# Windowed attention into a routed two-layer MLP: the order of all work from a list schedule, and most matmuls on the full array

## The chip, the core and the metric

The kernel runs on one core of a Trainium2 chip. The engines are TensorE (PE, with its weight loads shown apart as PEld), VectorE (DVE), ScalarE (ACT), GpSimd (POOL) and SyncE (SP), each of which works through its own instructions in order; 16 DMA engines move data between the device memory and the on-chip memory. The metric is the device time of one execution in microseconds (us). Lower is better.

## What is computed

Eight batches, eight heads, 576 tokens, head size 64. Each token attends to the tokens at most 32 places away. The heads are laid side by side into x (576 x 512 for a batch), x is pooled over its tokens, a gate picks one of eight experts for the whole batch, and the expert's two matrices are applied.

```python
    scores = scale * np.matmul(q, k.transpose(0, 1, 3, 2))
    mask = np.abs(pos[:, None] - pos[None, :]) <= window
    scores = np.where(mask, scores, -1000000000.0)
    scores = scores - np.max(scores, axis=-1, keepdims=True)
    attn = np.exp(scores)
    attn = attn / (np.sum(attn, axis=-1, keepdims=True) + 1e-09)
    return np.matmul(attn, v).astype(np.float32)
    ...
    pooled = x.mean(axis=1)
    logits = pooled @ w_gate
    e_idx = np.argmax(logits, axis=1)
    ...
        h = np.maximum(x[mask] @ w1[e], 0.0)
        out[mask] = gate_w[mask, None, None] * (h @ w2[e])
```

The inputs are q, k, v (8 x 8 x 576 x 64, float32, 9.4 MB each) and the weights w1 (8 x 512 x 1024) and w2 (8 x 1024 x 512), of which each batch reads one expert: 2.1 MB of each.

## The kernel before

The loop at the end of the program runs over the batches b: `attention(b)`, then `moe` of batch b-1, then `gate` of batch b. A library of tiles gives out the buffers (rotating pools) and puts in the waits; within each engine the instructions stand nearly in the order of the text, with the neighbouring stages drawn together where the pools allow it.

`attention(b)` loads q, k and v with SP in pieces of 128 tokens (L134, L138); for each token and head one run of 64 floats, 256 bytes, is read. DVE casts q and k to bf16 and v to fp16 (L148 to L153). TensorE transposes q and k, two heads at a time, 128 tokens per transpose and 64 in the last (L162), and DVE copies the result out of PSUM (L167). The keys are cut into blocks of 128, 128, 128, 128 and 64. For each block the scores against its window of at most 192 queries are accumulated on top of a mask: a matmul with the identity writes the mask (L185, 352 or 480 columns, all 128 rows of the array), and matmuls on 64 rows of the array, one head on the upper and one on the lower half, add the scores (L194). ACT takes the exponential from PSUM into `etile` (L203). For each block of queries, `avp` collects the products with `vaug` (v and a column of ones, 65 columns) from up to three key blocks (L221); the neighbouring blocks give 32 queries each, so these matmuls use 32 columns of the array. DVE divides by the row sum (L232, L235), TensorE transposes the result (L245), ACT copies it into `xTt` (L250).

`gate` pools with a DVE reduction (L255), multiplies with `w_gate` (L261), and finds the expert with a few tiny DVE instructions. `moe` has SP read the expert's number (L302) and load the two matrices as float32 (L304, L308); DVE casts them to fp16 (L312, L314); TensorE does the first layer, 64 matmuls of 288 columns (L322 and L326, one half of the tokens each), ACT applies the relu (L330, L333), TensorE does the second layer, 40 matmuls of 512 columns (L340), ACT scales by the gate's weight (L347) and SP stores (L351).

## Time and profile before

| | |
|---|---|
| time, median of 3 runs | 389.33 us (384.39 to 390.08) |
| span of the profiled execution | 384.9 us |
| PE busy | 307.4 us (80%), 2656 matmuls |
| PEld busy | 176.6 us (46%) |
| DVE busy | 165.9 us (43%) |
| ACT busy | 153.8 us (40%) |
| POOL busy | 7.9 us (2%) |
| moved by DMA | 71.74 MB in 130861 packets, 113936 of them under 512 bytes |
| mean granted TensorE clock | 0.852 of full speed |

The profiled execution is one execution of its own; its span runs from its first to its last instruction, and the times of the runs are taken apart from it. A busy PE is not a PE at its peak: a matmul counts as busy from its issue to its modelled end, and the clock of TensorE is granted at one of two levels, full (2.4 GHz) or half (1.2 GHz). An engine's idle time costs only where the chain of work that ended last passes through it.

### The profile page before, as it was taken

How to read it: one execution, taken by the hardware profiler on the slowest of the kernel's cores; microseconds unless marked ns; L12 is line 12 of the kernel's file. 1: busy time of each engine (PE TensorE's matmuls, PEld its weight loads, DVE VectorE, ACT ScalarE, POOL GpSimd, SP SyncE). 2: the span in 40 equal slices, each digit the busy share in tenths (PEclk: the TensorE clock that was granted, in tenths of full speed). 3: DMA queues.
4: the chain of work that ended last, by engine and by line, in shares of the span. 5: the costliest groups of instructions: out<-in, count | busy, mean ns of one | idle time of the engine just before them, and what ended most of it. 6: DMA issues, size and time to landing. Idle time of an engine off the chain costs nothing.

```text
span 384.9 us, 6511 instructions
## 1 busy us (share of the span) xinstructions
PE 307.4 (80%) x2656; PEld 176.6 (46%) x2656; DVE 165.9 (43%) x349; ACT 153.8 (40%) x353; POOL 7.9 (2%) x31
## 2 busy tenths in 40 slices
PE   0397498699958997699969997799859995893395
PEld 0234244474445554475345554565337444551262
DVE  0634562651467153652476055633385046501310
ACT  1044126163622536153723455253716362352052
POOL 1400000000000000000000000000000000000000
PEclk9998558589995999599986997599978999598599
DMA  9999049905889189936897289927996495015803
GB/s 160 210 208 162 3 157 346 202 7 160 278 273 212 51 219 381 222 67 179 305 285 161 83 236 371 195 48 211 345 258 119 149 292 218 0 54 181 325 0 124
DMA packets 130861, 71.74 MB, mean 186 GB/s; under 512 B 113936, under 2 KB 113936, under 8 KB 130832
## 3 DMA queue, kind: packets, MB, share of 16 engines
q1 hardware_dynamic: 130832, 71.33, 70.6%
q8 instruction: 21, 0.34, 0.4%
q14 instruction: 8, 0.07, 0.1%
HBM read 61.88 MB, written 9.44 MB: 185 GB/s over the span
## 4 chain that ended last, share of the span: by engine, by line
PE 70%; DVE 17%; DMA 6%; issue 4%; POOL 1%; SPq 0%; ACT 0%; DVEq 0%; POOLq 0%; ACTq 0%
PE op L340 18%; PE hpa L322 11%; PE hpb L326 10%; PE tp L162 8%; PE spAB L185 7%; PE avp L221 6%; PE spAB L194 6%; DVE xs L235 5%; DMA w2s<-in_moe_w_dram 4%; DVE w1s L312 4%; DVE w2s L314 4%; PE xtp L245 4%; DMA w1s<-in_moe_w_dram 2%; DVE linv L232 2%; DVE kbf L148 1%
## 5 line engine op out<-in xcount | busy, mean ns | idle before, releaser
L322 PE MATMUL hpa<-xTt,w1s 128*128 128x288 f16 x256 | 77.3, 331 | 12.2 <-DVE w1s L312 12.2
L326 PE MATMUL hpb<-xTt,w1s 128*128 128x288 f16 x256 | 76.6, 328 | 0.0
L203 ACT ACTIVATE etile<-spAB 128x480 f16<-128x480 f32 (+1 forms) x128 | 54.7, 550 | 48.3 <-PE spAB L194 47.4
L340 PE MATMUL op<-w2s,hT 128*128 128x512 f16 (+1 forms) x320 | 71.3, 380 | 0.0
L245 PE MATMUL xtp<-id_f,xs 128*128 128x128 f16 (+1 forms) x160 | 25.1, 254 | 41.0 <-DVE xs L235 40.2
L250 ACT COPY xTt<-xtp 128x512 f16<-128x512 f16 (+1 forms) x40 | 21.7, 542 | 83.2 <-PE xtp L245 83.2
L340 PEld LDWEIGHTS <-hT 128*128 128x128 f16 (+1 forms) x320 | 31.4, 100 | 37.2 <-issue 3.4
L347 ACT ACTIVATE osb<-op,gwb 128x512 f32<-128x512 f32 (+1 forms) x40 | 27.4, 686 | 43.7 <-PE op L340 43.7
L221 PE MATMUL avp<-vaug,etile 128*32 128x65 f16 (+3 forms) x832 | 44.9, 212 | 0.0
L330 ACT ACTIVATE hT<-hpa 128x288 f16<-128x288 f32 x64 | 26.2, 410 | 42.7 <-PE hpa L322 42.7
L221 PEld LDWEIGHTS <-etile 128*32 128x32 f16 (+3 forms) x832 | 37.1, 110 | 5.8 <-issue 1.6
L322 PEld LDWEIGHTS <-w1s 128*128 128x128 f16 x256 | 28.6, 112 | 23.0 <-DVE w1s L312 12.3
L266 DVE COPY lg<-lgp 1x8 f32<-1x8 f32 x8 | 1.2, 154 | 86.3 <-PE lgp L261 86.2
L232 DVE RECIPROCAL linv<-avp 128x8 f32<-128x8 f32 (+1 forms) x40 | 8.1, 203 | 67.1 <-PE avp L221 67.1
L245 PEld LDWEIGHTS <-xs 128*128 128x128 f16 (+1 forms) x160 | 9.8, 104 | 55.8 <-DVE xs L235 52.6
L326 PEld LDWEIGHTS <-w1s 128*128 128x128 f16 x256 | 28.5, 111 | 10.5
L235 DVE TENSOR_TENSOR xs<-avp,linv 128x256 f16<-128x256 f32 (+1 forms) x80 | 30.1, 417 | 1.4
L194 PE MATMUL spAB<-qTs,kTs 64*128 64x192 bf16 (+2 forms) x320 | 29.0, 249 | 0.0
L162 PE MATMUL tp<-id_bf,qbf 128*128 128x128 bf16 (+1 forms) x160 | 17.3, 236 | 14.3 <-DVE qbf L148 12.8
L333 ACT ACTIVATE hT<-hpb 128x288 f16<-128x288 f32 x64 | 25.9, 405 | 0.0
L255 DVE TENSOR_REDUCE pooledT<-xTt 128x4 f32<-128x2304 f16 x8 | 20.4, 2553 | 11.3 <-ACT xTt L250 11.3
L194 PEld LDWEIGHTS <-kTs 64*128 64x128 bf16 (+1 forms) x320 | 11.4, 97 | 29.8 <-issue 27.0
(51 smaller groups left out, 220.3 us busy)
## 6 DMA issues: line engine op xcount, KB each, us to landing
w1s<-in_moe_w_dram SPq DMA_DIRECT2D x8, 2048.0 KB, 8.1
w2s<-in_moe_w_dram SPq DMA_DIRECT2D x8, 2048.0 KB, 13.3
raw_q<-in_q_dram SPq DMA_DIRECT2D x32, 256.0 KB, 7.3
raw_k<-in_k_dram SPq DMA_DIRECT2D x32, 256.0 KB, 5.2
raw_v<-in_v_dram SPq DMA_DIRECT2D x32, 256.0 KB, 3.6
out_dram<-osb SPq DMA_DIRECT2D x32, 256.0 KB, 2.2
raw_q<-in_q_dram SPq DMA_DIRECT2D x8, 128.0 KB, 5.1
raw_k<-in_k_dram SPq DMA_DIRECT2D x8, 128.0 KB, 4.9
```

The source lines that it names most:

```text
L162: nc.tensor.transpose(tp[:, SO[t] : SO[t] + ST[t]], src[0 : ST[t], t, 2 * hp : 2 * hp + 2, :], id_bf[0 : ST[t], 0 : ST[t]],)
L185: nc.tensor.matmul(sp[h][:, 0:mw], id_bf, ma, start=True, stop=False, skip_group_check=True,)
L194: nc.tensor.matmul(sp[h][0:J, off : off + RL[kb]], kTs[hoff : hoff + D, hp, KO[kb] : KO[kb] + J], qTs[hoff : hoff + D, hp, RLO[kb] : RHI[kb]],
L203: nc.scalar.activation(et[h][:, eo : eo + mw], sp[h][:, 0:mw], mybir.ActivationFunctionType.Exp, bias=0.0, scale=0.125,)
L221: nc.tensor.matmul(avp[pr : pr + m, base : base + 65], Es[h][0:J, EOFF[kb] + lo : EOFF[kb] + lo + m], vaug[0:J, kb, h, :], start=(ci == 0 ...
L235: nc.vector.tensor_tensor(xs[0:stl, bk * 256 : (bk + 1) * 256].rearrange("p (h4 d) -> p h4 d", h4=4), hv[:, bk, :, 0:64], linv[0:stl, bk, ...
L245: nc.tensor.transpose(xtp[:, dt, 0:stl], xs[0:stl, dt * P : (dt + 1) * P], id_f16[0:stl, 0:stl],)
L322: nc.tensor.matmul(hpa, lhs, xTt[:, dt, 0:N1A], start=(dt == 0), stop=(dt == NDT - 1),)
L326: nc.tensor.matmul(hpb, lhs, xTt[:, dt, N1A:S], start=(dt == 0), stop=(dt == NDT - 1),)
L330: nc.scalar.activation(hT[:, ft, 0:N1A], hpa, mybir.ActivationFunctionType.Relu)
L340: nc.tensor.matmul(op[0:stl, :], hT[:, ft, SO[t] : SO[t] + stl], w2s[:, ft, :], start=(ft == 0), stop=(ft == NFT - 1),)
L347: nc.scalar.activation(osb[0:stl, :], op[0:stl, :], mybir.ActivationFunctionType.Copy, bias=0.0, scale=gwb[0:stl],)
```

## The change

The kernel's body is written anew. Four things change.

**The order.** Every piece of work is an `Op` with an engine, a length put in by the author, the ops it waits for, the buffers it takes and frees, and a priority. `Plan.finish` runs once when the program is built: it keeps a clock for each engine and always emits the op that can start first (at equal time that of the lower priority), so that attention of later batches and the two layers of earlier ones are dealt out among each other. The priority of the layers of batch b is that of batch b + 1.4. The lengths decide the order only; on the chip every engine runs its list in order and waits on semaphores.

**The shapes.** Pairs of heads (h, h + 1) are laid behind one another, 1152 tokens that divide into nine full blocks of 128: all transposes of q and k are 128 x 128. The mask is no longer a matmul: the scores are written alone, ACT takes the exponential, and DVE multiplies with a mask of zeros and ones. `E` has blocks of zeros beside each band (the zero gaps), so that the products with v always use 128 stationary columns, two matmuls for each head and block of queries; the blocks of queries are shifted by 32. The pooling is 20 one-column matmuls. The last block of the second layer (64 tokens) runs as two halves of 256 columns side by side on 64 columns of the array each.

**Who does what.** q and k are loaded nine tokens to a partition (2304 bytes in one run), v as before in runs of 256 bytes, one DMA for each batch. POOL casts q, k and v (in batch 0 DVE casts k). The weights are loaded by POOL's own DMA queue, which converts them to fp16 on the way; the DVE casts are gone. Copies out of PSUM go to DVE or ACT, whichever the schedule finds free.

**The buffers.** All tiles live through the whole program and are handed on by the plan: 6 halves of raw q or k, 2 of raw v, 2 of `E`, 2 each of w1 and w2, 3 of the output, five PSUM banks for attention (`psA`) and three for the layers (`psM`).

The core of the diff; all of the old body (printed above) goes away.

```diff
--- before.py
+++ after.py
 ...
+    LAT = {"PE": 0.2, "ACT": 0.12, "DVE": 0.12, "SP": 0.0, "SW": 0.2}
+    DMA_GBS = 370.0
+    SOON = 0.08
 ...
+            if best is None:
+                raise RuntimeError(f"nothing can start: {[(e, [o.name for o in r]) for e, r in ready.items()]}")
+            _, t, op, eng = best
+            for e in op.eng.split("/"):
+                ready[e].remove(op)
+            op.eng = eng
+            left -= 1
+            for res, n in op.takes:
+                have = sorted(self.free[res], key=lambda h: h[:2])
+                got, self.free[res] = have[:n], have[n:]
+                op.got[res] = [g[2] for g in got]
+                held[(op.name, res)] = got
+            op.emit(op)
+            end = at[op.eng] = t + op.dur
+            over = end + self.LAT[op.eng]
+            if op.land:
+                dma_at = max(dma_at, end + 1.3) + op.land / (self.DMA_GBS * 1e3)
+                over = dma_at + 0.7
 ...
+    buffers("raw", [P, 2, J, D], FP32, 6)
+    buffers("qkb", [P, J, 2, D], BF16, 4)
+    qTs = buffers("qT", [P, 2 * QPAD + 2 * S], BF16, 4)
+    buffers("kT", [P, 2 * S], BF16, 4)
+    vraws = buffers("vraw", [P, 36, D], FP32, 2)
+    vaugs = buffers("vaug", [P, 36, D + 1], FP16, 2)
+    Es = buffers("E", [P, H, EH], FP16, 2)
+    buffers("xs", [P, DM], FP16, 7)
+    buffers("xT", [P, NDT, S], FP16, 3)
+    buffers("w1", [P, NDT, F], FP16, 2)
+    buffers("w2", [P, NFT, DM], FP16, 2)
+    buffers("hT", [P, S], FP16, 9)
+    buffers("osb", [P, DM], FP32, 3)
+    banks = [ps.tile([P, 512], FP32, name=f"bank{i}") for i in range(8)]
+    plan.resource("psA", banks[0:5])
+    plan.resource("psM", banks[5:8])
 ...
+                    nc.sync.dma_start(
+                        t.rearrange("p h j d -> p h (j d)"),
+                        src[b, 4 * quad : 4 * quad + 4]
+                        .rearrange("(h x) s d -> (x s d) h", h=2)
+                        .rearrange("(p r) h -> p h r", p=P),
+                    )
+                plan.add("SP", 0.6, f"ld{name}{b}{quad}", load, takes=[("raw", 1)],
+                         deps=[f"W2{b - 2}_"] if b > 1 else [],
+                         land=650e3, prio=base + quad)
 ...
+                    t = op.got["qkb"][0]
+                    (nc.vector if op.eng == "DVE" else nc.gpsimd).tensor_copy(
+                        t, raw[(b, quad, name)].rearrange("p h j d -> p j h d")
+                    )
+                    raw[(b, quad, name)] = t
+                plan.add("DVE" if b == 0 and name == "k" else "SW", 1.2, f"c{name}{b}{quad}", cast,
 ...
+            vr_of[b] = t
+            nc.sync.dma_start(
+                t, v[b].rearrange("h s d -> (h s) d").rearrange("(j p) d -> p j d", p=P)
 ...
+                        bank_of[tn] = bank
+                        pv = bank.bitcast(BF16).rearrange("p (j c) -> p j c", c=P)
+                        for j in range(j0, j1):
+                            nc.tensor.transpose(
+                                pv[:, j - j0, :], raw[(b, quad, name)][:, j], id_bf
+                            )
+                    plan.add("PE", 0.056 * (j1 - j0), tn, tr,
+                             deps=[f"c{name}{b}{quad}"] + ([f"T{b}{quad}{name}0"] if part else [])
+                             + (["ca"] if b == 0 else []),
 ...
+                        bank_of[sn] = bk
+                        kt, qt = qkT[(b, quad, "k")], qkT[(b, quad, "q")]
+                        for n in range(2):
+                            u = 2 * half + n
+                            k0 = pp * S + 128 * u + 64 * pp
+                            for h2 in range(2):
+                                rows = slice(64 * h2, 64 * h2 + 64)
+                                nc.tensor.matmul(
+                                    bk[h2][:, 192 * n : 192 * n + 192],
+                                    kt[rows, k0 : k0 + 128],
+                                    qt[rows, QPAD + k0 - 32 : QPAD + k0 + 160],
+                                    start=True, stop=True, skip_group_check=True,
+                                )
+                    pr = base + 100 + 250 * half + 40 * (2 * quad + pp)
+                    plan.add("PE", 0.40, sn, score,
+                             deps=[f"CT{b}{quad}{n}{p}" for n in "qk" for p in range(2)]
+                             + ([f"S{b}000_"] if quad + pp + half else []),
 ...
+                        ev = E_of[b].rearrange("p (a h x) c -> p a x h c", a=2, h=2)
+                        ev = ev[:, quad, pp, :, 512 * half : 512 * half + 512]
+                        ev = ev.rearrange("p h (u c) -> p h u c", c=256)[:, :, :, 0:192]
+                        mm = mask[:, pp : pp + 1, 2 * half : 2 * half + 2]
+                        nc.vector.tensor_tensor(
+                            ev, ev, mm.broadcast_to([P, 2, 2, 192]), ALU.mult
+                        )
+                    plan.add("DVE", 0.47, f"M{b}{quad}{pp}{half}", msk,
+                             deps=[f"X{sn}{h}" for h in range(2)] + (["cb"] if b == 0 else []),
 ...
+                        first_slot = (9 * h - par) // 2
+                        if i == 4:
+                            if par == 0:
+                                parts = [(ESH + 64, 4), (0, 0)]
+                            else:
+                                parts = [(896, 4), (ESH - 32, 0)]
+                        elif par == 0:
+                            parts = [(256 * i + 64, i),
+                                     (256 * (i + 1) - 64 if i < 3 else ESH - 64, i + 1)]
+                        else:
+                            parts = [(256 * i, i + 1),
+                                     (256 * (i - 1) + 128 if i else ESH + 32, i)]
+                        for n, (c0, t) in enumerate(parts):
+                            nc.tensor.matmul(
+                                bank[:, hp * 65 : hp * 65 + 65],
+                                E_of[b][:, h, c0 : c0 + 128],
+                                va_of[b][:, first_slot + t, :],
+                                start=(hp == 0 and n == 0), stop=(n == 1),
+                                skip_group_check=True,
+                            )
+                last = i == NQT - 1 and par == 1
 ...
+                for i in range(NQT):
+                    nc.tensor.matmul(
+                        bank[:, dt : dt + 1],
+                        xs_of[(b, i)][:, dt * P : (dt + 1) * P],
+                        onet if i == NQT - 1 else onec,
+                        start=(dt == 0 and i == 0), stop=(i == NQT - 1),
+                        skip_group_check=True,
+                    )
 ...
+            ereg = nc.gpsimd.value_load(tiny("idx", [1, 8], U32, b)[0:1, 0:1], min_val=0, max_val=NE - 1)
+            w1s = op.got["w1"][0]
+            w_of[b] = [w1s, None, ereg]
+            nc.gpsimd.dma_start(
+                w1s, moe_w1[ds(ereg, 1)][0].rearrange("(dt p) f -> p dt f", p=P)
+            )
+        plan.add("SW", 1.6, f"W1{b}", loadw, deps=[f"G{b}"], takes=[("w1", 1)], land=2.2e6,
 ...
+                            bank[:, 0:288], w_of[b][0][:, dt, ft * P : (ft + 1) * P],
+                            xT_of[b][:, dt, 288 * c : 288 * c + 288],
+                            start=(dt == 0), stop=(dt == NDT - 1),
+                        )
+                last = ft == NFT - 1 and c == 1
+                before = [moe_last[0] + "_"] if moe_last else []
+                moe_last[:] = [gn]
+                plan.add("PE", 0.49, gn, g1,
+                         deps=before + [f"W1{b}"] + [f"CR{b}{i}" for i in range(NQT)],
+                         takes=[("psM", 1)],
 ...
+                        if i < 4:
+                            nc.tensor.matmul(
+                                bank, h_of[(b, ft)][:, 128 * i : 128 * i + 128], w2s[:, ft, :],
+                                start=(ft == 0), stop=(ft == NFT - 1),
+                            )
+                            continue
+                        for c in range(2):
+                            nc.tensor.matmul(
+                                bank[64 * c : 64 * c + 64, 0:256],
+                                h_of[(b, ft)][:, 512:576],
+                                w2s[:, ft, 256 * c : 256 * c + 256],
+                                start=(ft == 0), stop=(ft == NFT - 1),
+                                tile_position=(0, 64 * c), skip_group_check=True,
+                            )
+                before = [moe_last[0] + "_"]
 ...
```

How the instructions stand on three engines, before and now.

TensorE, the scores of one pair of heads in a middle batch, before: `spAB` are the two PSUM banks of the pair, `maA` and `maB` the masks, `kTs` the transposed keys.

```order
L185 LDWEIGHTS id_bf_63
L185 MATMUL spAB_1170<-maA_82,id_bf_63 128x352
L185 LDWEIGHTS id_bf_63
L185 MATMUL spAB_1171<-maA_82,id_bf_63 128x352
L194 LDWEIGHTS kTs_1111
L194 MATMUL spAB_1170<-qTs_1110,kTs_1111 128x160
L194 LDWEIGHTS kTs_1111
L194 MATMUL spAB_1171<-qTs_1110,kTs_1111 128x160
```

TensorE, scores of a middle batch, now: `w10` holds the first matrix of an earlier batch's expert, `xT2` that batch's tokens.

```order
L400 LDWEIGHTS kT2_79
L400 MATMUL bank3_116<-qT2_75,kT2_79 128x192
L400 LDWEIGHTS kT2_79
L400 MATMUL bank2_115<-qT2_75,kT2_79 128x192
L650 LDWEIGHTS w10_97
L650 MATMUL bank7_120<-xT2_96,w10_97 128x288
```

The mask matmuls are gone, and groups of the first layer of an earlier batch stand between the groups of scores.

DVE, between the products with v and the layers of a middle batch, before: `w1s32` and `w2s32` are the loaded weights, `avp` the products.

```order
L235 TENSOR_TENSOR xs_1871<-avp_1844,linv_1833 128x256 x2
L312 CAST w1s_1993<-w1s32_1989 128x4096
L232 RECIPROCAL linv_1905<-avp_1880 128x8
L235 TENSOR_TENSOR xs_1907<-avp_1880,linv_1905 128x256 x2
L232 RECIPROCAL linv_1941<-avp_1916 128x8
L235 TENSOR_TENSOR xs_1943<-avp_1916,linv_1941 128x256 x2
L314 CAST w2s_1995<-w2s32_1991 128x4096
```

DVE at the same place now (`E1` are the exponentials, `mask_129` the zeros and ones, `xT0` the transposed result):

```order
L521 RECIPROCAL linv010_353<-bank0_113 128x4
L523 TENSOR_TENSOR xs5_92<-bank0_113,linv010_353 128x4x64
L432 TENSOR_TENSOR E1_86<-E1_86,mask_129 128x2x2x192
L294 COPY xT0_94<-bank2_115 128x4x128
L432 TENSOR_TENSOR E1_86<-E1_86,mask_129 128x2x2x192
L521 RECIPROCAL linv100_391<-bank4_117 128x4
L523 TENSOR_TENSOR xs6_93<-bank4_117,linv100_391 128x4x64
```

The two long casts left DVE's list; the masks and some copies came in.

The weights of a middle batch, before, on SP (the expert's number, the two loads, then the next batch's q):

```order
L302 TENSOR_LOAD lgi_1070
L304 ISA
L304 DMA w1s32_1438<-in_moe_w1_dram 128x4x1024
L308 ISA
L308 DMA w2s32_1440<-in_moe_w2_dram 128x8x512
L134 DMA raw_q_1633<-in_q_dram 128x8x64 x4
```

Now, on POOL, between the casts of q, k and v:

```order
L319 CAST qkb2_71<-raw2_65 128x1152
L319 CAST qkb3_72<-raw3_66 128x1152
L617 TENSOR_LOAD idx2_1349
L617 ISA x2
L620 ISA
L620 DMA w10_97<-in_moe_w1_dram 128x4x1024
L629 ISA
L629 DMA w20_99<-in_moe_w2_dram 128x8x512
L637 ISA gwb2_1410<-gw2_1391 128x1
L341 CAST vaug1_84<-vraw1_82 128x18x64 x2
```

The read of the expert's number (the row with `idx2`) now stands in the list of the engine that also casts the next batch's inputs.

## Rows read from the trace of the kernel before

**Rows 1.** Windows: length; busy us (instructions) PE, PEld, DVE, ACT, POOL; clock; DMA share; GB/s.

```profile
180.42:223.32 42.90, 37.51 (x334) 21.56 (x334) 20.28 (x43) 19.00 (x45) 0.26 (x1) 0.88 0.76 209
265.62:306.92 41.30, 35.92 (x334) 20.82 (x335) 20.28 (x43) 19.00 (x45) 0.26 (x1) 0.92 0.82 217
```

**Rows 2.** Chain of waits in order of time, one batch: start us, length us, engine, line.

```profile
180.42 3.69 PE tp L162 x40
184.12 0.41 PE spAB L185 x2
184.52 0.26 PE spAB L194 x4
184.78 0.51 PE spAB L185 x2
...
192.78 0.78 PE avp L221 x24
...
194.58 2.20 DVE w1s L312
...
200.04 2.20 DVE w2s L314
...
204.79 0.24 PE hpb L326
...
210.26 0.12 PE hpb L326
...
214.30 8.75 PE op L340 x40
```

**Rows 3.** Windows view, three short stretches, columns as in rows 1.

```profile
8.00:12.00 4.00, 0.00 (x0) 0.00 (x0) 1.82 (x4) 0.00 (x0) 3.14 (x11) 1.00 1.34 207
204.00:208.00 4.00, 4.00 (x19) 2.50 (x20) 3.36 (x2) 1.79 (x5) 0.00 (x0) 0.50 1.04 217
354.00:362.00 8.00, 0.09 (x1) 0.10 (x2) 2.29 (x1) 0.00 (x0) 0.00 (x0) 0.50 1.02 398
```

**Rows 4.** Groups by line: operation, shapes, count, busy us, mean ns, idle before, releaser.

```profile
L203 ACT ACTIVATE etile<-spAB 128x480 f16<-128x480 f32 (+1 forms) x128 | 54.7, 550 | 48.3 <-PE spAB L194 47.4
L235 DVE TENSOR_TENSOR xs<-avp,linv 128x256 f16<-128x256 f32 (+1 forms) x80 | 30.1, 417 | 1.4
L347 ACT ACTIVATE osb<-op,gwb 128x512 f32<-128x512 f32 (+1 forms) x40 | 27.4, 686 | 43.7 <-PE op L340 43.7
L330 ACT ACTIVATE hT<-hpa 128x288 f16<-128x288 f32 x64 | 26.2, 410 | 42.7 <-PE hpa L322 42.7
L250 ACT COPY xTt<-xtp 128x512 f16<-128x512 f16 (+1 forms) x40 | 21.7, 542 | 83.2 <-PE xtp L245 83.2
L167 DVE COPY qTs<-tp 128x576 bf16<-128x576 bf16 x32 | 14.2, 443 | 2.1 <-PE tp L162 1.0
L232 DVE RECIPROCAL linv<-avp 128x8 f32<-128x8 f32 (+1 forms) x40 | 8.1, 203 | 67.1 <-PE avp L221 67.1
```

**Rows 5.** Timeline of the start: start us, length us, engine, line, operation [idle before, releaser].

```profile
10.71 0.34 POOL L82 TENSOR_SCALAR_AFFINE_SELECT maB_f<-maB_f 128x192 f32<-128x192 f32 x1
11.37 1.35 DVE L148 CAST qbf<-raw_q 128x2048 bf16<-128x2048 f32 x1
11.60 1.32 POOL L82 TENSOR_SCALAR_AFFINE_SELECT maB_f<-maB_f 128x192 f32<-128x192 f32 x1
12.78 0.82 PE L162 MATMUL tp<-id_bf,qbf 128*128 128x128 bf16 x6 [12.78 <-DVE qbf L148]
```

**Rows 6.** DMA issues: tile, queue, count, KB each, median us from issue to landing.

```profile
w1s<-in_moe_w_dram SPq DMA_DIRECT2D x8, 2048.0 KB, 8.1
w2s<-in_moe_w_dram SPq DMA_DIRECT2D x8, 2048.0 KB, 13.3
out_dram<-osb SPq DMA_DIRECT2D x32, 256.0 KB, 2.2
```

More of the change, by code (lines that the diff above doesn't have):

```diff
@@ L15 @@
 U32 = mybir.dt.uint32
[L16 removed]
+ACTF = mybir.ActivationFunctionType
+ALU = mybir.AluOpType
 B = 8
@@ new lines, in pool @@
+        def pool(op):
+            bank = op.got["psA"][0]
+            bank_of[f"P{b}"] = bank
+            for dt in range(NDT):
+                for i in range(NQT):
+                    nc.tensor.matmul(
+                        bank[:, dt : dt + 1],
[3 more added lines that the diff above has]
+                        skip_group_check=True,
+                    )
@@ new lines, in add_batch, with poolc, logits @@
+        plan.add("PE", 0.6, f"P{b}", pool, deps=[f"NA{b}4{p}" for p in range(2)] + [f"R{b}4"],
+                 takes=[("psA", 1)],
+                 frees=[(f"NA{b}{i}0", "xs") for i in range(NQT)], prio=base + 930)
+        def poolc(op):
+            pooled = tiny("pooled", [P, NDT], FP32, b)
+            nc.vector.tensor_copy(pooled, bank_of.pop(f"P{b}")[:, 0:NDT])
+        plan.add("DVE", 0.12, f"CP{b}", poolc, deps=[f"P{b}"], frees=[(f"P{b}", "psA")],
+                 prio=base - 900)
+        def logits(op):
+            bank = op.got["psA"][0]
+            bank_of[f"L{b}"] = bank
+            pooled = tiny("pooled", [P, NDT], FP32, b)
+            for dt in range(NDT):
@@ L353, with choose @@
-    prev = None
-    for b in range(B):
-        xTt = attention(b)
-        if prev is not None:
-            moe(*prev)
-        lgi, gwb = gate(xTt)
-        prev = (xTt, lgi, gwb, b)
-    moe(*prev)
+        plan.add("PE", 0.45, f"L{b}", logits, deps=[f"CP{b}", "wg"], takes=[("psA", 1)],
+                 prio=base - 900)
+        def choose(op):
+            lg = tiny("lg", [1, NE], FP32, b)
+            nc.vector.tensor_scalar_mul(lg, bank_of.pop(f"L{b}")[0:1, 0:NE], 1.0 / S)
+            top = tiny("top", [1, 8], FP32, b)
+            nc.vector.max(top, lg)
+            idx = tiny("idx", [1, 8], U32, b)
+            nc.vector.max_index(idx, top, lg)
+            negm = tiny("negm", [1, 1], FP32, b)
+            nc.vector.tensor_scalar_mul(negm, top[:, 0:1], -1.0)
```

696 lines of the change are left out of this document (420 added, 276 removed).

## Prediction

> **What bounds the kernel now.** I read the windows of whole batches first, then the chain of waits through one batch, then the groups by line, and the DMA last.
>
> A batch in the middle takes 42.9 or 41.3 us, and PE is busy for 37.5 or 35.9 of them, DVE for 20.3, ACT for 19.0 [rows 1]. So PE is the engine to look at: it idles for 5.4 us of each batch, and its mean clock of 0.88 says that it spent 24% of the batch, some 10 us, at half clock, which costs 5 us more. The chain [rows 2] shows what fills the rest. 40 transposes take 3.69 us, 92 ns each; 512 columns take 8.75 / 40 = 219 ns, which is 0.427 ns a column, so that 128 columns alone would be 55 ns. Each pair of mask matmuls takes 0.41 us for 704 columns (0.30 us by that rate) or 0.51 us for 960 (0.41): some 0.1 us goes to the change between the full array and its half-row form, and there are sixteen such changes in a batch. The two weight casts of 2.20 us each stand on the chain, since the divisions (L232, L235) wait behind them on DVE. After that idle stretch the layers begin at half clock: 0.24 us a matmul where it is 0.12 us later, and the granted clock of 204 to 208 us is 0.50 [rows 2, 3]. DMA is busy at a share of 0.76 to 0.82 [rows 1]; the 256-byte runs alone occupy it wholly at 207 GB/s, where the weights pass at 398 GB/s [rows 3].
>
> **The change, priced.** *TensorE, per batch at full clock* (0.427 ns a column, [rows 2]): 36 transposes 1.97; 20 transposes of x 1.09; scores, eight groups of 4 x 192 and one of 8 x 96 columns. Four score matmuls of 160 columns took 0.26 us [rows 2], and two columns run side by side there (two heads), 2 x 160 x 0.427 = 0.14, so 0.12 is the change of form; a new group is 2 x 192 x 0.427 + 0.12 + 0.10 = 0.39, nine groups 3.5. Products with v: 24 took 0.78 us, 33 ns each [rows 2], 80 make 2.6. Pooling, 20 of one column at the same 33 ns, and the gate: 1.0. Together attention costs 10.1 us. First layer 64 x 288 x 0.427 = 7.9, second 32 x 512 x 0.427 = 7.0, the last block as two halves side by side 8 x 256 x 0.427 + 0.2 = 1.1: 16.0 us. The sum is 26.1 us a batch, against 42. The upper bound takes 92 ns for each transpose of q and k (+1.3) and the last block's halves one after the other (+0.9): 28.3.
>
> *ACT*, whole kernel: 144 exponentials of 384 columns at 0.55 (the mean of 352 and 480 columns, an upper price) = 79; 128 relus x 0.410 = 52; 32 x 0.686 + 8 x 0.41 (half the columns, priced as a relu) = 25; the 45 copies that fall to it at 0.542 to 0.69 (542 scaled to 640 columns) = 24 to 31 [rows 4]. With the gate some 190 us, 24 a batch: under PE, by little.
>
> *DVE*, whole kernel: 80 x 0.417 + 80 x 0.203 = 50 for the divisions; 33 copies x 0.443 to 0.50 and 26 to `xT` = 27; 72 mask multiplications of 768 elements, for which no row stands: below, the 576 elements of L167 scaled, 0.59; above, the 0.417 of 256 elements from PSUM scaled, 1.25 [rows 4]. I take 0.6, since both operands lie on chip as 16-bit data as in L167: 43. With the gate 130 us, 16 a batch; at the upper end 177, 22 a batch. Neither reaches PE.
>
> *POOL*, 30 casts of 1152 and 16 of as many elements. The nearest rows are its own 192 columns in 0.34 us and DVE's 2048 in 1.35 [rows 5]: between 0.76 and 2.0 us each. I take 1.3, 60 us in all, 7.5 a batch, and at 2.0 it is 12. The issue of the weight loads comes to that. All of it is under 26 as work, but not as order: the read of the expert's number waits for the gate, and behind it in POOL's list stand the casts of the next batch, which the transposes wait for. The list puts them after a batch that is already cast, so I price this wait at nothing at best and as a rival below.
>
> *DMA, per batch*: weights 4.2 MB at 398 GB/s = 10.5; q and k, now in runs of 2304 bytes, 2.36 MB at the same rate 5.9 (at 207: 11.4); v, still 256 bytes, 1.18 MB at 207 = 5.7; output 3.0 [rows 3]. 25.1 us, nearly as much as PE. No row shows a load that converts on the way; below it is the 398 GB/s of the plain load, above it the 207 GB/s of short runs (+9.7 us a batch). I take 398, since the reads are as long as before.
>
> *Start.* PE began at 12.78 us [rows 5], behind q whole. Now half of q and half of k (0.59 MB each) are enough: DMA begins at 2 us, the first cast is at about 5, PE at 7.5. Loads of the first batch end at 2 + 5.9 + 5.7 = 14, casts of v at 18; ACT needs 18 x 0.55 + copies from 9.5 on, until 22; ten divisions at 0.62 after that, the pooling and the gate: the expert of batch 0 is known at 29.5, the load goes out at 31, lands 8.1 us later [rows 6], with other loads beside it 3 later: the first layer of batch 0 begins at **42**. Until then PE has done two attentions but for 2 us; half clock there costs nothing, since ACT and DMA set the pace.
>
> *Sum.* 42 + 2 + six attentions 60.6 + eight times the layers 128 = 232.6. At the end PE has 7.2 us of batch 6's second layer while batch 7's gate (1.5), issue (1.0) and landing (8.1) pass: 3.4 of waiting. Last scaling and store 0.69 + 2.2 [rows 4, 6]. 239 without any other wait. For waits I take half of the 5.4 us that PE idles in a batch now [rows 1], because groups of the layers stand between the steps of attention, over six batches: 16. **255 us** of span. The old profiled span is 384.9 against a median of 389.3 and a lowest time of 384.4; I add half of that gap: **257 us**.
>
> *A rule against it.* In the timeline of the start, a POOL instruction that takes 0.34 us alone took 1.32 beside a DVE cast of 1.35 that began just before it [rows 5]. The Trainium skill (SBUF — State Buffer, Who interferes with whom) says that DVE and GpSimd hold one pair of ports for a whole instruction and the other blocks, also while GpSimd writes the descriptors of its own DMAs; the row agrees. The change sends the casts and the weight loads to POOL and gives DVE masks whose two operands both lie on chip, so this is a rival; its price, worked out below from rows, would be by the rule as by the row: one whole instruction a time.
>
> **Rivals.**
> *Clock.* TensorE falls to half clock in every attention, as it does now. For: long runs of transposes and short products remain. Against: groups of the layers stand among them, and in the middle of the old layers the clock is full. Price 5 us in each of six batches: 287.
> *Ports and POOL's list.* Each of nine mask multiplications in a batch waits for a POOL cast, or the cast for it, 0.6 to 1.0 us a time as in rows 5, and the weight load is issued late by as much: 5 to 9 us a batch, 34 us and more in six: 291 to 305. For: rows 5. Against: POOL is busy for only 7.5 of 26 us.
> *Converting load at 207 GB/s.* DMA then needs 35 us a batch and is the bound: 42 + 7 x 35 + 16 + 3 = 306, up to 340 with waits.
> *Slower than before.* The same load, slower still: place, POOL's queue; 397 us is passed when a batch takes (397 - 61) / 7 = 48 us, of which 14.6 are the other transfers, so at 33 us for 4.2 MB, 126 GB/s. Only a rate under that decides it, and no row is that low.
> *Better.* The layers start at 36, and the waits are 4 us: 237 or less.
> *The order does not hold.* The list is made from lengths put in by hand; where one is wrong, an engine waits in order. That is contained in the 16 us, and at twice that gives 271.
>
> **How the numbers follow.** Chances: PE-paced, 240 to 275, 0.60; clock 0.10; ports and POOL 0.12; load at about 207 GB/s 0.08; under that, slower than before, 0.04; better than 240, 0.06. The predicted time is the first case. The range of 236 to 305 leaves out the load cases and half of the better one, some 0.15. 2% (about what a measurement can tell from no change) is 8 us: faster 0.93, within 0.03, slower 0.04.
>
> **What would show it.** In the new profile: a batch of 26 to 29 us in the windows; PE at a clock of 0.95 or more after 42 us; PE's first wait for w1 ending near 42; no wait of PE for DVE casts; DMA share near 0.9. It is wrong if PE's longest waits end with w1 or w2 in every batch (the converting load or POOL's list), if POOL's casts take over 2 us, or if the transposes take 92 ns without changes of form.

## The result and the profile after

The changed kernel takes **262.95 us** (262.94 to 263.43, four runs) against 389.12 for the kernel before on the same chip: a ratio of **0.680** (95% interval 0.675 to 0.684). 257.0 was predicted, 236 to 305 the range. The profiled execution has a span of 261.3 us.

Busy time by engine, and the two busy DMA queues (q0 is POOL's converting loads, q1 is SP's; packets, MB written, share of 16 engines' span), page of the kernel after:

```profile
PE 223.8 (86%) x2528; PEld 148.0 (57%) x2528; DVE 146.8 (56%) x418; ACT 163.7 (63%) x374; POOL 71.1 (27%) x74
q1 hardware_dynamic: 24720, 37.77, 48.2%
q0 software_dynamic: 12544, 16.78, 38.9%
```

Windows of the kernel after (columns as in rows 1): until the first layer of batch 0, one batch in the middle, five batches in the middle (each from one batch's last block of the second layer to the next batch's), and from there to the end.

```profile
0.00:44.50 44.50, 27.19 (x340) 19.58 (x341) 37.81 (x123) 26.19 (x56) 20.21 (x21) 0.91 1.00 268
66.90:93.40 26.50, 25.85 (x319) 17.20 (x318) 15.70 (x41) 18.66 (x43) 8.72 (x9) 1.00 1.07 259
66.90:208.20 141.30, 133.43 (x1583) 87.76 (x1584) 85.57 (x226) 98.26 (x230) 44.62 (x45) 0.98 1.01 243
231.80:261.30 29.50, 19.17 (x129) 11.37 (x128) 0.00 (x0) 10.63 (x23) 0.00 (x0) 0.90 0.57 134
```

Five batches take 141.3 us, 28.3 each, where one took 41.3 to 42.9 [rows 1]. PE is busy for 26.7 of them at a clock of 0.98: it is nearly full. DMA's share is 1.01, but a share adds up the times of packets that overlap and reaches 1.34 [rows 3], so it does not say how full DMA is; the runs below do. In the best batch PE does all its work in 25.9 us at full clock.

What PE, and in the last row ACT, waited for in the kernel after (us in total, times, longest):

```profile
PE bank L650 <- DMA w<-in_moe_w_dram: 7.0, 3, 4.9
PE bank L361 <- POOL qkb L319: 6.2, 1, 6.2
PE bank L361 <- DVE qkb L319: 4.3, 1, 4.3
PE bank L537 <- DVE xs L523: 3.9, 6, 2.4
ACT osb L711 <- DMA out_dram<-osb: 10.6, 6, 3.7
```

The second and third stand in the first 12 us. The wait for the weight casts on DVE is gone. Of the weights, the 4.9 us is the end of the kernel. The last row is new, and shows how DMA reaches PE in the middle; the chain of waits has it twice there and once at the end (start us, length us, what; the rows from 172.19 to 173.33 serve a point further down):

```profile
72.88 0.98 PE bank L650 x8
73.86 0.55 PE bank L502 x16
...
82.24 0.58 PE bank L361 x10
...
86.83 7.26 DMA out_dram<-osb
...
94.19 0.69 ACT osb L711
94.88 1.14 ACT E L419 x3
...
144.45 7.79 DMA out_dram<-osb
152.34 0.69 ACT osb L711
...
172.19 0.86 PE bank L685 x4
173.06 0.27 PE bank L400 x4
173.33 0.97 PE bank L685 x4
...
200.24 10.85 DMA w<-in_moe_w_dram
211.14 0.66 PE bank L650 x4
...
227.70 10.01 DMA w<-in_moe_w_dram
...
252.70 3.76 DMA out_dram<-osb
...
256.57 0.47 ACT osb L711
```

These two stores took 7.26 and 7.79 us behind the weights (a median of 6.7 over all, 2.2 before [rows 6]); with three output buffers, ACT's next scaling waited for them, and the exponentials of another batch, which TensorE needed, stood behind that scaling in ACT's list. The weights stand on the chain in the middle too; where the row of 10.85 us ends, PE had waited for them for 1.5 us.

Changes are compared by medians, with the ratio to the kernel before on the same chip; the profiled executions of e5_before_conv, g1_start, g2_end and g4_all were the longest of their runs (1.5 to 3.2% over the shortest), that of e4_half_weights was the shortest (253.11 us), and that of e8_stages_short was disturbed and is not read.

### The profile page after: what moved, and what is told of

Its sections match the earlier page's. It is cut to its first block, busy times and chain, and to the rows that moved or that the text cites. A ratio compares the mean times of both kernels' runs of the same rounds, so it can differ in the third digit from the quotient of the medians.

```text
span 261.3 us, 6394 instructions
## 1 busy us (share of the span) xinstructions
PE 223.8 (86%) x2528; PEld 148.0 (57%) x2528; DVE 146.8 (56%) x418; ACT 163.7 (63%) x374; POOL 71.1 (27%) x74
## 3 DMA queue, kind: packets, MB, share of 16 engines
q1 hardware_dynamic: 24720, 37.77, 48.2%
q0 software_dynamic: 12544, 16.78, 38.9%
## 4 chain that ended last, share of the span: by engine, by line
PE 52%; DMA 19%; DVE 13%; ACT 9%; issue 3%; SPq 1%; POOLq 1%; ACTq 0%; DVEq 0%
PE bank L650 24%; DMA w<-in_moe_w_dram 12%; PE bank L685 8%; DMA out_dram<-osb 7%; PE bank L502 6%; PE bank L361 5%; ACT E L419 4%; DVE E L432 4%; PE bank L537 4%; DVE xs L523 2%; PE bank L400 2%; PE bank L560 1%; ACT hT L667 1%; SPq L726 1%; ACT osb L711 1%
## 5 line engine op out<-in xcount | busy, mean ns | idle before, releaser
L650 PE MATMUL bank<-xT,w 128*128 128x288 f16 x512 | 79.9, 297 | 10.1 <-DMA w<-in_moe_w_dram 7.0
L667 ACT ACTIVATE hT<-bank 128x288 f16<-128x288 f32 x128 | 52.8, 414 | 43.1 <-PE bank L650 39.2
L685 PE MATMUL bank<-w,hT 128*128 128x512 f16 x256 | 63.9, 380 | 0.0
L432 DVE TENSOR_TENSOR E<-E,mask 128x768 f16<-128x768 f16 x64 | 45.5, 717 | 30.2 <-ACT E L419 30.1
L650 PEld LDWEIGHTS <-w 128*128 128x128 f16 x512 | 47.8, 101 | 24.2 <-DMA w<-in_moe_w_dram 7.9
L319 POOL CAST qkb<-raw 128x1152 bf16<-128x1152 f32 x30 | 37.2, 1250 | 78.2 <-DMA raw<-in_q_dram 41.4
L419 ACT ACTIVATE E<-bank 128x384 f16<-128x384 f32 x128 | 54.3, 503 | 6.2 <-PE bank L400 5.3
L523 DVE TENSOR_TENSOR xs<-bank,linv 128x256 f16<-128x256 f32 x80 | 34.0, 425 | 2.7
L502 PE MATMUL bank<-vaug,E 128*128 128x65 f16 x640 | 30.3, 201 | 0.7 <-ACT E L419 0.3
L502 PEld LDWEIGHTS <-E 128*128 128x128 f16 x640 | 27.7, 103 | 4.5 <-DVE E L432 1.4
L294 DVE COPY xT<-bank 128x512 f16<-128x512 f16 (+1 forms) x26 | 10.2, 393 | 14.7 <-PE bank L537 14.4
```

The costliest lines, as they stand in the source:

```text
L319: (nc.vector if op.eng == "DVE" else nc.gpsimd).tensor_copy(t, raw[(b, quad, name)].rearrange("p h j d -> p j h d"))
L419: nc.scalar.activation(dst.rearrange("p (u c) -> p u c", c=256)[:, :, 0:192], bank_of[sn][h2][:, 0:384].rearrange("p (u c) -> p u c", c=19 ...
L432: nc.vector.tensor_tensor(ev, ev, mm.broadcast_to([P, 2, 2, 192]), ALU.mult)
L502: nc.tensor.matmul(bank[:, hp * 65 : hp * 65 + 65], E_of[b][:, h, c0 : c0 + 128], va_of[b][:, first_slot + t, :], start=(hp == 0 and n == ...
L523: nc.vector.tensor_tensor(xv[:, par], hv[:, :, 0:64], linv.to_broadcast([P, 4, 64]), ALU.mult)
L650: nc.tensor.matmul(bank[:, 0:288], w_of[b][0][:, dt, ft * P : (ft + 1) * P], xT_of[b][:, dt, 288 * c : 288 * c + 288], start=(dt == 0), st ...
```

## The experiments

Two theories: **PE** (a batch is TensorE's 26 us at full clock, attention hides in the layers because of the order) and **DMA** (28 us of transfers, added up from the queues' shares, set the batch), beside the rivals of the prediction.

### Order undone: e1_stages

```diff
-                         deps=before + [f"W1{b}"] + ...
+                         deps=([f"P{b + 1}"] if b < B - 1 and ft + c == 0 else []) + before + ...
...
-                             + (["ca"] if b == 0 else []),
+                             + (["ca"] if b == 0 else []) + ([f"2{b - 2}40_"] if b > 1 else []),
```

> The changed kernel with its dealing-out undone: the first layer of batch b waits for the pooling of batch b+1, and the transposes of batch b+2 wait for the last block of the second layer of batch b, so that TensorE does attention and layers in turn, as before the change; shapes, engines and buffers stay. Theory PE (the batch is TensorE's 26 us of work at full clock, and the order lets attention hide in the layers): attention alone is paced by ACT and DVE and the steps between engines, 17 to 20 us a batch, and the layers 16, so 44.7 + 16 + 6 x 33 to 36 + 16 + 5 = 280 to 298 us. Theory DMA (28 us of transfers set the batch): the same 280 to 298, with a DMA share that falls to about 0.8. Rival, the new shapes give all of the gain and the order none: under 270 us.

Measured: 302.88 us (ratio 0.786, 0.781 to 0.791). Windows of one attention stage, one stage of the layers, and the next attention stage:

```profile
102.70:121.50 18.80, 14.52 (x198) 10.53 (x197) 15.13 (x35) 12.26 (x27) 7.30 (x6) 0.73 0.89 245
121.50:137.70 16.20, 16.20 (x126) 10.24 (x122) 1.09 (x9) 8.78 (x21) 1.94 (x3) 1.00 1.12 252
137.70:156.50 18.80, 14.59 (x198) 10.30 (x197) 15.70 (x35) 12.09 (x27) 7.57 (x6) 0.73 0.54 154
```

This is 5 us above the 280 to 298 that both theories expected. The batch is 18.8 + 16.2 = 35.0 us: the layers at their forecast 16, attention paced by DVE and ACT and the steps between them. Undoing the order alone costs 40 us of the 126. It does not tell the two theories apart, but "the order gives nothing" falls.

### Mask as a matmul again: e2_mask_matmul

```diff
+                        for h2 in range(2):
+                            nc.tensor.matmul(
+                                bk[h2][:, 0:384], id_bf, madd[:, pp, 2 * half : 2 * half + 2],
+                                start=True, stop=False, skip_group_check=True,
+                            )
...
-                        nc.vector.tensor_tensor(
-                            ev, ev, mm.broadcast_to([P, 2, 2, 192]), ALU.mult
-                        )
```

> The changed kernel with the mask again as a matmul: two identity matmuls of 384 columns ahead of each of the nine groups of scores of a batch, DVE's mask multiplications gone. TensorE has 2 x 384 x 0.427 ns = 0.33 us more in each group, 2.95 us a batch, 23.6 us in all. Theory PE: 270 to 287 us (lower end if the 2.2 us that TensorE idles in a batch swallow most of it). Theory DMA: the work fits into idle time, at most 8 us more, under 271. Rival, ports (a mask multiplication and a POOL cast wait for each other, and TensorE waits for both): the waits go away and the time falls below 262.

Measured: 269.89 us (0.702, 0.697 to 0.707): 7 us for 23.6 us of columns. That is at the lower end of theory PE, but also within theory DMA's "under 271", so the time does not decide between them; the window of one batch does:

```profile
97.50:126.90 29.40, 29.00 (x335) 18.51 (x334) 10.45 (x34) 21.09 (x49) 8.77 (x9) 1.00 0.96 236
```

TensorE is busy for 29.0 of 29.4 us at full clock, and DMA's share is lower than before: now TensorE is the bound and nothing else. The first layer begins at 43.8 us, no later than without the added columns, so the 5.9 us of them in the first two attentions are hidden; of the rest, most took up idle time and half clock (28.3 us a batch became 29.5 in the mean of five). DVE was relieved at the same time (10.5 us in this window, 15.7 above), so this run does not say whether the order or DVE's relief paid for the columns; the pairs below do for the staged order.

### Half of the weights: e4_half_weights

```diff
+            n = NDT if b < 2 else NDT // 2
-                w1s, moe_w1[...]
+                w1s[:, 0:n], moe_w1[...][:, 0:n]
```

(and the same for w2)

> The changed kernel, but from batch 2 on only half of each weight matrix is loaded (the other half is what an earlier batch left, so that part of the result of batches 2 to 7 is computed from old weights); the order of all work stays. DMA has 6.3 us less in each of six batches, 22 in place of 28. Theory PE: the batch stays at 26.1 of work plus waits; only the wait for the last weights (4.9 us) and some small ones go: 250 to 260 us. Theory DMA: six batches of 22 to 23 would fall under the work of TensorE, so each comes down to 26.1: 262.9 - 6 x 2.2 - 4.9 = 245 or less, and waits in the middle vanish.

Measured: 256.72 us (0.670, 0.666 to 0.674), theory PE. Batches of 26.4, 27.2, 26.7, 26.8 and 31.3 us follow each other (26.5, 29.7, 28.0, 28.1 and 29.0 in the kernel after); the first, the third and the last as windows:

```profile
65.50:91.90 26.40, 25.63 (x317) 17.08 (x316) 15.48 (x42) 20.02 (x47) 8.91 (x9) 1.00 1.08 262
119.10:145.80 26.70, 25.95 (x319) 17.18 (x319) 17.01 (x47) 19.13 (x45) 6.89 (x8) 1.00 0.82 200
172.60:203.90 31.30, 28.65 (x317) 18.98 (x316) 17.57 (x46) 19.62 (x46) 8.59 (x9) 0.89 0.63 163
```

With DMA at 0.82 the batch comes to 26.7, TensorE's own work. PE's waits for the weights fall from 7.0 to 1.2 us, ACT's for output buffers from 10.6 to 1.9. So DMA's queueing costs 1.3 us in a batch, in the mean of the first four, and 3.7 at the end; it does not set the batch. The fifth batch got longer, and not by DMA: at its start TensorE waits 2.5 us for ACT and DVE, and then, by the clock of 0.89, runs some 7 us at half clock. With it the gain is 0.6 us a batch.

### q and k in short runs: e3_short_runs

```diff
-    buffers("raw", [P, 2, J, D], FP32, 6)
+    buffers("raw", [P, J, 2, D], FP32, 6)
...
-                        t.rearrange("p h j d -> p h (j d)"),
+                            t[:, :, h],
```

(one DMA for each pair of heads)

> The changed kernel with one part undone: q and k come in runs of 256 bytes again (as v does), in place of 2304 bytes; everything else stays. At the 207 GB/s of rows 3 their 2.36 MB a batch occupy DMA for 11.4 us where they now take 6.7, so DMA needs 28 + 4.7 = 32.7 us a batch and passes TensorE's 26.1. If DMA then sets the batch: 262.9 + 6 x (32.7 - 28.3) + 2 to 5 at the start = 290 to 295 us, with a DMA share of 1 throughout. Rival, transfers are hidden anyway: under 268.

Measured: 296.6 us (0.769, 0.760 to 0.777), just above what DMA as the bound would give. Queue and waits (as above):

```profile
q1 hardware_dynamic: 90768, 37.77, 56.6%
```

```profile
PE bank L362 <- POOL qkb L320: 18.1, 8, 7.4
```

The split was not as expected: the first layer begins at 55.7 us (11 later, not 2 to 5), and a batch takes 30.6 us from first layer to first layer (27.6 in the kernel after), not 32.7. That the total came so near is therefore luck in part, and the run does not show DMA as the bound of a batch. The long runs are worth 34 us in this order.

### q and k cast by DVE: e6_cast_dve

```diff
-                plan.add("DVE" if b == 0 and name == "k" else "SW", 1.2, f"c{name}{b}{quad}", cast,
+                plan.add("DVE", 1.2, f"c{name}{b}{quad}", cast,
```

> The changed kernel with all casts of q and k on DVE in place of POOL (the order is made anew from the same lengths). Theory PE: DVE then has 147 + 26 x 1.3 - 9 (mask multiplications back at 0.56 us) = 170 us of 262, still under TensorE, so the time stays within 2%, 258 to 268. Rival, ports (casts on POOL and mask multiplications on DVE hold each other up, and TensorE pays): the mean of a mask multiplication falls from 0.72 to about 0.58 us and the time falls by 1 us or more a batch, under 255. Rival, DVE's list becomes the path: 275 or more, with waits of TensorE for DVE.

Measured: 273.21 us (0.705, 0.697 to 0.713): slower by 10 us, past both first expectations and just short of the third. Mask multiplication by line, and PE's longest wait:

```profile
L432 DVE TENSOR_TENSOR E<-E,mask 128x768 f16<-128x768 f16 x64 | 37.9, 597 | 28.0 <-ACT E L419 28.0
```

```profile
PE bank L650 <- DMA w<-in_moe_w_dram: 18.2, 6, 5.1
```

The masks do get shorter (0.717 to 0.597 us), but the casts on DVE take 1.34 us each, and TensorE now waits for weights in six batches, not three. DVE's list is the dearer place for them. That the gate's steps on DVE come later behind the casts, and the weights with them, fits; it was not tried by itself.

### The weight casts alone taken from the old kernel: e5_before_conv

```diff
-        w1s32 = moew.tile([P, NDT, F], FP32, name="w1s32", tag="mw32", bufs=3)
-        nc.sync.dma_start(
-            w1s32, moe_w1...
+        w1s = moew.tile([P, NDT, F], FP16, name="w1s", tag="mw16", bufs=3)
+        nc.gpsimd.dma_start(
+            w1s, moe_w1...
...
-        nc.vector.tensor_copy(w1s, w1s32)
```

(the same for w2; the read of the expert's number moves from SP to POOL with the loads)

> The kernel before with one part of the change alone: the weights are loaded by POOL's converting queue straight to fp16, and DVE's two casts of 2.2 us per batch are gone. Theory of the prediction (the casts stand on the chain, divisions wait behind them): 8 x 4.4 = 35 us less, 350 to 360. Rival (something else is late at the same place, such as the landing of the weights, which now come at 331 GB/s in place of 398, or the TensorE clock): 375 to 390.

Measured: 396.94 us (1.029, 1.021 to 1.038), **slower** than before: both theories missed. From TensorE's first transposes to the next batch's, batches took 46.6, 48.2, 41.3, 41.2, 51.0 and 41.2 us (before: 46.3, 43.4, 42.2, 42.9, 42.3, 41.3). Chain of waits of the batch of 51.0:

```profile
238.68 7.30 SPq L134
...
246.02 8.58 DMA raw_v<-in_v_dram
...
254.72 1.23 DVE vaug L152
```

Three batches gain 0.1 to 1.7 us, not 4.4. In those of 48.2 and 51.0 v of the next batch was issued right behind the weights, which no longer stand in SP's queue ahead of it, and came late; DVE's cast of v stands ahead of a division, and everything waited. The stretch before the first of these batches is 4.8 us longer too (40.5 and not 35.7), for which no cause was looked for. POOL's issue of the weight loads, beside DVE's casts and in the last batch alone:

```profile
234.89 1.69 POOL L304 DMA_DIRECT2D w1s<-in_moe_w_dram  x1 [1.27 <-DVE kTs L167]
366.85 0.79 POOL L304 DMA_DIRECT2D w1s<-in_moe_w_dram  x1 [1.19 <-issue]
```

### Three pairs: e7_stages_mask, e9_stages_both, e8_stages_short

e7_stages_mask is the edits of e1_stages and e2_mask_matmul together; e9_stages_both puts DVE's multiplications (the lines with - in e2_mask_matmul) back into it; e8_stages_short is e1_stages and e3_short_runs.

> The stages in turn (as in e1_stages) and the mask as a matmul (as in e2_mask_matmul) together. If the dealt order is what hid most of the mask matmuls in e2_mask_matmul (7 us measured for 23.6 us of columns), the same matmuls cost their whole price where attention stands alone: six batches at 2.95 us, some of it at half clock, 302.9 + 18 to 30 = 321 to 333 us. If it was the relief of DVE that paid for them, they cost no more here than there: 302.9 + 0 to 8 = 303 to 311.

Measured: 297.97 us (0.769, 0.763 to 0.775). That is 5 us *faster* than e1_stages with 23.6 us more on TensorE, below what either side expected. Its attention stages run at full clock, where those of e1_stages had 0.73, and e9_stages_both was made to tell clock and relief apart.

> As e7_stages_mask (stages in turn, mask as a matmul), with DVE's mask multiplications put back beside the mask matmuls (they multiply by ones where it matters and zeros by zero), so that TensorE does the work of e7_stages_mask and DVE that of e1_stages. If the mask matmuls made e7_stages_mask faster than e1_stages by keeping TensorE's clock up: attention stays at a clock of 0.95 or more, about 17 us a stage, and the time is 296 to 302 us. If they did so by relieving DVE: the granted clock of attention falls again, a stage takes 19 us or more, and the time is 305 to 325, over e1_stages by what the added columns cost.

Measured: 314.21 us (0.815, 0.811 to 0.820). Attention and layers of e7_stages_mask, and then, below them, attention and layers of e9_stages_both:

```profile
99.60:116.50 16.90, 14.20 (x217) 8.64 (x216) 8.74 (x26) 12.23 (x27) 6.67 (x6) 0.99 0.78 209
116.50:134.10 17.60, 17.60 (x128) 10.83 (x125) 1.07 (x9) 8.79 (x21) 1.95 (x3) 0.91 1.12 263
```

```profile
106.40:125.20 18.80, 14.90 (x215) 8.95 (x214) 15.56 (x35) 12.23 (x27) 7.57 (x6) 0.97 0.67 193
125.20:143.90 18.70, 18.70 (x127) 11.30 (x124) 1.10 (x9) 8.90 (x21) 1.94 (x3) 0.85 1.14 251
```

The time and the stage are those of the second expectation, the clock is that of the first. The clock is 0.97 and the stage is 18.8 us all the same, as in e1_stages: DVE's 15.6 us and the steps around it set it, and DVE's relief (8.7) is what made the attention of e7_stages_mask shorter. The expected fall of the clock within attention did not come: a stretch at half clock stands in the layers instead, in both kernels (0.91 and 17.6 us, 0.85 and 18.7 us, where e1_stages had 1.00 and 16.2). Half clock cost nothing where DVE paced the stage (18.8 us at 0.73 and at 0.97), and its price where TensorE did.

> The stages in turn (as in e1_stages) and q and k in runs of 256 bytes (as in e3_short_runs) together. A staged batch takes 35 us and DMA then needs 32.7, so if the bound of a batch is the longer of the two, the short runs, which cost 34 us in the dealt order, cost here only the start, 2 to 8 us: 305 to 311. If they cost by contention or by late landings in any order: 320 or more.

Measured: 316.88 us (0.818, 0.812 to 0.824): 14 us over e1_stages, between the two expectations. The short runs cost less than half of the 34 us that they cost in the dealt order, but more than the start; what the rest is stays open.

### The ends: g1_start, g2_end, g4_all

```diff
-    plan.add("DVE", 2.5, "cb", constants_b, deps=["ca"], prio=30)
+    plan.add("DVE", 2.4, "cb", constants_b, deps=["ca"], prio=30)
+    plan.add("DVE", 2.8, "cb2", constants_b2, deps=["cb", "ck01_"], prio=30)
```

(g1_start: `constants_b2` is the part on `mshort`)

> The changed kernel with the constants of DVE split in two, so that the casts of k of batch 0 stand ahead of the mask constants of the short blocks (3.0 us of DVE work) instead of behind them. If that order is why the first layer began at 44.7 and not at 42: TensorE's wait for DVE's cast falls from 4.3 to about 2 us, the gate of batch 0 and the first layer come 2 to 3 us earlier, and the time is 260 to 261. If v, ACT or the weights set that point: 262 to 264.

Measured: 263.13 us (0.675, 0.665 to 0.685). The single runs lie between 260.07 and 265.34, over both expectations, so the time does not decide. The trace says more: the wait for DVE's cast fell to 1.8 us, the gate's matmuls of batch 0 came at 32.4 and not 33.5, and the first weights were issued at 35.1 and not 36.1, but they landed after 8.9 us and not 8.0, and the first layer, which now waited for them, began at 44.0 and not 44.5.

```diff
-        mo = base + int(LAG * 1000)
+        mo = base + int((2.0 if b == B - 2 else LAG) * 1000)
...
+            n = 2 if b in (0, B - 1) else 1
+            for c in range(n):
+                s = slice(c * F // n, (c + 1) * F // n)
```

(g2_end: w1 of the first and last batch in `n` loads)

> The changed kernel with two edits at the ends: the layers of batch 6 get the priority of batch 8 in place of 7.4, so that the gate of batch 7 stands ahead of more of them, and the first matrix of batches 0 and 7 is loaded in two halves of its columns, so that the first layer can begin on the first half. If the landing of the last weights is on the path (4.9 us of waiting), and that of the first (2.3 us): 255 to 259 us, and TensorE's waits for w fall from 7.0 to under 3. If the gate of batch 7 can't come earlier, since its loads and casts set it: 260 to 263.

Measured: 261.51 us (0.674, 0.666 to 0.683), the second expectation; the interval also holds the ratio of the changed kernel. The longest wait for weights fell from 4.9 to 2.7 us, their sum not at all (7.1). The gate of batch 7 was not earlier (225.5 us; 225.4 before the edit).

> The changed kernel with the edits of g1_start and g2_end together, and with the last batch's block of 64 tokens computed first instead of last, so that the kernel does not end with its four small stores (5 us behind the last matmul now, of which about 2 would go). If the ends are worth what their waits show: 255 to 258 us. If each gain is taken back by the next late thing (the landing of the weights, which share DMA with the next loads): 259 to 263.

Measured: **257.93 us** (0.663, 0.659 to 0.668, seven runs; `for i in (4, 0, 1, 2, 3)` in the last batch), the upper end of the first expectation: 5 us under the changed kernel, and its interval lies below that one's. Waits for weights are 1.9 us in its profile. The three edits together are worth about 5 us. What each adds is not shown: neither g1_start nor g2_end is clear of noise by itself, and the block of 64 tokens was not put first alone.

## Why the prediction was right, point by point

**TensorE's work, 26.1 us a batch: right.** 25.9 us in the best batch. Piece by piece from the chain: first layer 8 in 0.98 (forecast 123 ns each), 16 products with v in 0.55 (34 ns, forecast 33), 10 transposes in 0.58 (58 ns, forecast 55). A group of four score matmuls takes 0.27 and makes the four matmuls of the second layer behind it take 0.97 in place of 0.86, so 0.38 with the change of form (forecast 0.39).

**Period: right, its waits by luck.** 26.1 + 16/6 = 28.8 us forecast, 28.3 measured. The 16 us of waits were half of an old figure and not worked out from any wait of the new kernel, so that they fit is luck. What fills them: over the five batches PE idles 7.9 us, and in two of them the clock is 0.94, some 3.5 us at half clock each. A part is DMA, by ACT's waits for output buffers: in e4_half_weights the first four batches fall from 28.1 to 26.8 us in the mean. The fifth rose there from 29.0 to 31.3 with TensorE waiting for ACT and DVE, so a part is not DMA.

**Where the 6.3 us of span went** that it has over the forecast 255: the start 2.5 (44.5, not 42; the first weights were issued at 36.1 and not at 31, but landed in 8.0 us and not in 11, so two larger errors cancel in part), the last weights 1.5 (4.9, not 3.4: landing 10.0 us, not 8.1), behind the last matmul 2.1 (5.0, not 2.9: a wait for an output buffer, then four small stores). From the first layer on, without the two ends: 206.9 us measured, 206.6 forecast. The 2 us from span to median were 1.7.

**The start.** DVE's constants stood ahead of the cast of k (timeline of the kernel after, DVE first and then POOL; the first row is a mask constant, the masks of DVE and the rows of POOL serve the point on the ports below):

```profile
8.70 1.49 DVE L251 CAST mshort<-ones 64x96 f16<-64x96 f32 x4
10.21 1.35 DVE L319 CAST qkb<-raw 128x1152 bf16<-128x1152 f32 x1
...
17.53 4.49 DVE L432 TENSOR_TENSOR E<-E,mask 128x768 f16<-128x768 f16 x4
...
22.41 1.01 DVE L432 TENSOR_TENSOR E<-E,mask 128x768 f16<-128x768 f16 x2
```

```profile
16.07 2.25 POOL L341 CAST vaug<-vraw 128x1152 f16<-128x1152 f32 x2 [6.31 <-DMA vraw<-in_v_dram]
18.25 2.89 POOL L319 CAST qkb<-raw 128x1152 bf16<-128x1152 f32 x2
```

PE's wait for that cast, 4.3 us, goes against a sign named beforehand (no wait of PE for DVE casts). After the result this looked like the cause of the late first layer; g1_start shows that it is only the first late thing of several, since the landing of the weights took most of the gain back.

**DVE and ACT: sizes off, place right.** DVE 147 us (forecast 130), ACT 164 (190). The copies of q and k out of PSUM took 0.72 to 0.82 us on DVE where 0.443 to 0.50 was taken from L167 [rows 4]; they put five or four elements from as many transposes side by side in every nine of the target, where L167 copied straight. That this is why was only argued. Neither engine set the dealt batch as a whole. But DVE does set a staged one (e9_stages_both), so "neither reaches PE" held by the order.

**Mask off TensorE: the price was right, the worth was not in it.** The columns add what was priced to TensorE's work (25.9 us in the best batch, 29.0 in e2_mask_matmul) but cost only 7 us in all there, and in stages the mask as a matmul was the better choice (e7_stages_mask against e1_stages, 5 us).

**POOL and the ports.** POOL's casts took 1.25 us (forecast 1.3). In the rows above four masks beside POOL's casts took 1.12 us each, two without 0.51; over the kernel the mean is 0.717. Of the 64 masks of the long blocks, 24 overlap a POOL cast and take 0.99 us in the mean, 39 overlap no POOL instruction and take 0.55. Against 0.55 the mean is 12 us more for 72 masks, 1.5 us of DVE time a batch and not the 5 to 9 us of TensorE's that the rival needed. The Trainium skill (SBUF — State Buffer, Who interferes with whom) says that a DVE instruction with two inputs in SBUF contends with a GpSimd instruction that reads SBUF, and that GpSimd can be starved of port time for generating descriptors. The masks agree with the first, the issue of 1.69 us beside DVE's casts against 0.79 in e5_before_conv with the second. A mask beside an issue of weight loads was not slowed: 0.56 us for the one here, 0.53 to 0.56 for five in e6_cast_dve.

**DMA: the price of the converting load was right, and the shares mislead.** It was priced at 398 GB/s of bytes read. By the shares it looks slower: q0 took 38.9% of 261.3 us, 102 us for the 33.6 MB that it reads, 330 GB/s, and with q1's 126 us DMA comes to 28.4 us a batch and not 25.1. The 331 GB/s and the 28 us in the expectations of the experiments are such figures. But the times of packets overlap. Where the load runs alone (window of the kernel after; GB/s counts the bytes written, half of those read):

```profile
239.00:242.00 3.00, 2.85 (x15) 1.84 (x15) 0.00 (x0) 1.57 (x5) 0.00 (x0) 0.59 1.24 208
```

it reads 416 GB/s at a share of 1.24, and the first matrix of batch 0 landed 8.0 us after its issue, where the plain load took 8.1 [rows 6]. So the rival "load at 207" fell, and how near DMA is to its limit is told by e3_short_runs and e4_half_weights, not by the share.

**Clock.** 0.98 in the middle, as forecast for the dealt order (0.94 in two of five batches); the rival's fall in every attention is what e1_stages shows when the order is undone.

**A reading that failed.** "The two weight casts of 2.20 us each stand on the chain" is right as a row, but e5_before_conv gained 1.7 us a batch at most from their end. That run also moved the issue of the loads, so it does not price the casts alone. In the forecast this did no harm, since the new sum was made from TensorE's work and not as 389 less the parts.

## What to carry to other kernels

When the whole order is remade, add up the new bound's own work from rows and leave the old chain: a single part was worth 34 us or 7 us when it was undone in the new kernel, and less than nothing when it was put into the old one, by what else was full. Where two resources come out close to each other, the second can reach the first through a small buffer pool (three output buffers here; more were not tried): look for what stands behind that wait in an engine's list. Do not read a DMA share of 1 as full before you know what share a load reaches alone. Ask of every slow stretch, of the clock too, whether the engine in question paces that stage; only there does it cost.

## What had not been expected of the hardware

A DMA load on POOL's queue that converts float32 to fp16 passed alone as fast as the plain load of the same matrices, 416 GB/s read (239 to 242 us) against 398 [rows 3], though its packets' times add up to a share of 1.24 against 1.02. And TensorE with 3 us more of matmuls in an attention kept its full clock there (0.97 to 0.99, against 0.73) but then ran a part of the next layers at half clock (0.91 in e7_stages_mask, 0.85 in e9_stages_both). By these clocks a batch of e9_stages_both spent 6.7 us at half clock and one of e1_stages 10.2, and yet it was the slower one: the slow stretch got shorter, but it moved to where TensorE sets the pace.
